# Score bursts of three slots over six PSUM banks, tied into the second MLP layer of two batches ahead, and all eight banks for the first layer

**Chip, cores, metric.** One core of a Trainium2 chip. The metric is device time in microseconds (us), median of several runs of the whole kernel; lower is better.

## The reference

```python
# 8 batches, 12 heads, 448 tokens, 64 per head; model width 768, rank 32
q_n, k_n = q / |q|, k / |k|                     # per token and head
attn = softmax(q_n @ k_n.T / tau)
x = (attn @ v) with the heads side by side      # 8 x 448 x 768
u = x + (x.T @ U @ V).T                         # low-rank mixing of tokens
out = u + relu(u @ w_ch1) @ w_ch2               # MLP, 768 -> 3072 -> 768
```

## The kernel before

The kernel is written as a list of operations for a small planner. The planner places them in time, engine by engine, with its own estimates of durations, and the instructions are then emitted in that order. So each engine's order is fixed when the kernel is built. TensorE has several streams with priorities; the MLP is the last and fills what the others leave. Tokens of the 8 batches are cut into tiles of 128 that are shared between two batches, so even batches have three tiles in the MLP (384 columns in the first layer) and odd ones four (512).

PSUM has eight banks, handed out by rings. A ring is a list of bank groups in order of preference and the number of groups it may hold at a time:

```python
r_mm = bank_ring([(7,), (6,), (5,), (4,)], 3)        # MLP, transposes, U^T x, V^T products
r_av = bank_ring([(5,), (6,), (7,), (4,)], 2, (4, D + 8))   # attention times values
r_sc = bank_ring([(0, 1), (2, 3)], 2)                # scores: a slot of two heads takes two banks
```

A pair of heads has four slots (112 keys each). Scores go in bursts of two slots, that is, four matmuls: the two heads lie in the upper and the lower 64 rows and run side by side.

```python
BURST = 2
for c0 in range(0, SC, g):                           # SC = 4; g = 1 in batch 0, else BURST
    scs = [Slot(r_sc, ...) for _ in range(g)]
    def score():
        for n, sc in enumerate(scs):
            for hh in range(2):
                r = slice(D * hh, D * hh + D)        # 64 rows
                nc.tensor.matmul(out=sc.tile[:, hh, 0:S], lhsT=flat[r, ...], rhs=qkT.tile[r, ...])
    # ... then one exponential on ScalarE per slot, then attention times values per head
```

U^T x comes in two halves of the columns, four matmuls of 32 output columns each, side by side in the array; V^T products and the addition of x follow on VectorE. The MLP:

```python
for f in range(24):                                  # first layer: 6 matmuls into one bank
    mm = Slot(r_mm, 1)
    # ... relu on ScalarE or VectorE empties the bank
for group in groups:                                 # second layer: 24 matmuls into one bank
    mms = [Slot(r_mm, 1) for _ in group]             # batch 0: first three outputs at once
    # ... VectorE adds u and empties the bank
```

## Time and profile before

| | before |
|---|---|
| median time | 598.7 us |
| span of the profiled run | 597.0 us |
| TensorE busy | 586.4 us (98%) |
| score matmuls (L620), all batches | 384 |
| ScalarE, VectorE busy | 46%, 52% |

TensorE is the bound.

### The profile page before, as it was taken

Reading aid. Unit: us, or ns where it says so; the run is one execution under the profiler, and the core shown is the slowest. Engines: PE = TensorE matmul, PEld = TensorE weight load, DVE = VectorE, ACT = ScalarE, POOL = GpSimd, SP = SyncE. Lnnn points to the kernel's source line nnn. Section 1 sums busy time; section 2 is a strip of 40 time slices with the busy share of each in tenths; the row PEclk is TensorE's granted clock in tenths of the full one; section 3 lists DMA queues with packets and bytes.
Section 4 is the critical chain, followed back from the end, with each engine's and each line's share of the span. In section 5 each row is a group of like instructions: output and inputs, shape, how many; then the busy total and the mean of one; then the engine's idle time right before and its main releaser. Section 6 shows DMA issues by size and latency. Waiting matters only on the chain.

```text
span 597.0 us, 11650 instructions
## 1 busy us (share of the span) xinstructions
PE 586.4 (98%) x4878; PEld 329.4 (55%) x4878; DVE 308.8 (52%) x730; ACT 272.0 (46%) x441; POOL 73.7 (12%) x98
## 2 busy tenths in 40 slices
PE   7999999999999999999999999999999999999997
PEld 5555555544555555554445665556445666654565
DVE  6969849999988678658773354124401210110011
ACT  7977653566644566556563046704541025014300
POOL 7234220041300110030020000000000000000000
PEclk9999999999999999999999999999999999999999
DMA  9999995897895695795394121041003110310021
GB/s 154 200 206 192 209 134 112 97 137 110 77 159 101 92 105 72 133 129 94 50 78 97 53 56 22 14 80 33 10 0 63 45 40 1 94 40 1 1 53 54
DMA packets 132852, 50.68 MB, mean 85 GB/s; under 512 B 97728, under 2 KB 132800, under 8 KB 132800
## 3 DMA queue, kind: packets, MB, share of 16 engines
q0 software_dynamic: 71680, 25.73, 38.9%
q1 hardware_dynamic: 61056, 24.19, 21.1%
q8 instruction: 38, 0.62, 0.5%
q14 instruction: 14, 0.11, 0.1%
q10 hardware_dynamic: 64, 0.02, 0.0%
HBM read 52.25 MB, written 11.01 MB: 106 GB/s over the span
## 4 chain that ended last, share of the span: by engine, by line
PE 92%; DVE 3%; ACT 3%; DMA 1%; issue 0%; POOL 0%; ACTq 0%; POOLq 0%
PE bank L850 37%; PE bank L816 36%; PE bank L647 8%; PE bank L620 7%; ACT attn L628 2%; PE bank L740 1%; DMA qk_nat<-in_k_dram 1%; PE bank L448 1%; PE bank L704 1%; DVE xn L573 1%; DVE u_nat L754 1%; DVE O_sb L859 0%; DVE relu L841 0%; ACT sq L499 0%; DVE u_nat L751 0%
## 5 line engine op out<-in xcount | busy, mean ns | idle before, releaser
L816 PE MATMUL bank<-uT,w_sb 128*128 128x512 bf16 (+1 forms) x1152 | 233.2, 353 | 1.9 <-ACT uT L880 0.6
L850 PE MATMUL bank<-w_sb,relu 128*128 128x384 bf16 (+1 forms) x1368 | 231.0, 323 | 0.4 <-DVE O_sb L859 0.3
L633 ACT ACTIVATE attn<-bank 112x896 bf16<-112x896 f32 x176 | 152.6, 920 | 123.8 <-PE bank L620 84.1
L850 PEld LDWEIGHTS <-relu 128*128 128x128 bf16 x1368 | 129.3, 98 | 92.5 <-issue 12.8
L816 PEld LDWEIGHTS <-w_sb 128*128 128x128 bf16 x1152 | 108.4, 98 | 113.5 <-issue 20.4
L839 ACT ACTIVATE relu<-bank 128x512 bf16<-128x512 f32 (+1 forms) x139 | 75.6, 545 | 130.7 <-PE bank L816 128.8
L859 DVE TENSOR_TENSOR O_sb<-bank,u_nat 128x384 f32<-128x384 f32 (+1 forms) x57 | 31.1, 548 | 186.3 <-PE bank L850 161.9
L505 DVE TENSOR_REDUCE ss<-sq 112x8 f32<-112x512 bf16 x96 | 62.6, 672 | 2.4 <-ACT sq L499 2.2
L647 PEld LDWEIGHTS <-attn 112*128 112x128 bf16 x1536 | 55.7, 97 | 10.3 <-issue 3.3
L573 DVE TENSOR_TENSOR xn<-qk_nat,inv 112x512 bf16<-112x512 bf16 x91 | 59.1, 677 | 0.1
L620 PE MATMUL bank<-qkT 64*128 64x448 bf16 x384 | 58.1, 354 | 1.0 <-ACT qkT L880 0.5
L647 PE MATMUL bank<-v_nat,attn 112*128 112x65 bf16 x1536 | 58.6, 193 | 0.1
L841 DVE TENSOR_SCALAR relu<-bank 128x384 bf16<-128x384 f32 (+1 forms) x53 | 32.8, 619 | 35.9 <-PE bank L816 33.8
L656 DVE TENSOR_TENSOR X_sb<-bank,rd 128x256 bf16<-128x256 f32 x96 | 39.0, 416 | 1.5
L479 POOL DMA_DIRECT2D v_nat<-in_v_dram x32 | 29.8, 937 | 61.7 <-PE bank L647 49.2
L470 POOL DMA_DIRECT2D qk_nat<-in_q_dram x24 | 17.2, 718 | 156.1 <-DVE xn L573 132.9
L501 DVE TENSOR_TENSOR sq<-qk_nat 112x512 bf16<-112x512 bf16 x89 | 34.0, 412 | 0.0
L654 DVE RECIPROCAL rd<-bank 128x4 f32<-128x4 f32 x96 | 16.7, 176 | 29.2 <-PE bank L647 28.3
L754 DVE TENSOR_TENSOR u_nat<-bank,X_sb 128x384 bf16<-128x384 f32 (+2 forms) x45 | 22.5, 525 | 15.3 <-PE bank L740 14.9
L620 PEld LDWEIGHTS <-qkT 64*128 64x128 bf16 x384 | 12.0, 94 | 21.9 <-issue 18.5
L628 ACT ACTIVATE attn<-bank,inv 112x448 bf16<-112x448 f32 x32 | 17.4, 656 | 0.7 <-DVE inv L527 0.7
L470 POOL DMA_DIRECT2D qk_nat<-in_k_dram x24 | 16.8, 700 | 4.8 <-DMA w_sb<-in_moe_w_ch_dram 3.6
(52 smaller groups left out, 159.7 us busy)
## 6 DMA issues: line engine op xcount, KB each, us to landing
v_nat<-in_v_dram POOLq DMA_DIRECT2D x32, 168.0 KB, 6.2
qk_nat<-in_q_dram POOLq DMA_DIRECT2D x23, 224.0 KB, 6.5
qk_nat<-in_k_dram POOLq DMA_DIRECT2D x23, 224.0 KB, 7.5
w_sb<-in_moe_w_ch_dram POOLq DMA_DIRECT2D x4, 1152.0 KB, 21.0
w_sb<-in_moe_w_ch_dram POOLq DMA_DIRECT2D x8, 576.0 KB, 15.9
out_dram<-O_sb SPq DMA_DIRECT2D x15, 168.0 KB, 2.3
out_dram<-O_sb SPq DMA_DIRECT2D x16, 144.0 KB, 2.1
out_dram<-O_sb SPq DMA_DIRECT2D x16, 120.0 KB, 2.0
```

Of the source, the lines that this page charges most:

```text
L470: ops = [load(lambda i=i, src=src: nc.gpsimd.dma_start(out=ld.tile[:, i, lo:lo + h1 - h0, :], in_=src[b, h0:h1].rearrange("h (s c) d -> s ...
L501: nc.vector.tensor_mul(y, x, x)
L505: lambda i=i, a0=a0, a1=a1, sq=sq: nc.vector.reduce_sum(ss.tile[:, i, a0:a1, :].rearrange("p h c -> p (h c)"), sq.tile[:, 0:a1 - a0, :].re ...
L573: nc.vector.tensor_mul(dst, src, sc)
L620: nc.tensor.matmul(out=sc.tile[:, hh, 0:S], lhsT=flat[r, SCH * (c0 + n):SCH * (c0 + n) + 128], rhs=qkT.tile[r, SC:2 * SC, :].rearrange("p ...
L633: exps.append(plan.add(Op("ACT", act_t(2 * S, 0.08), lambda sc=sc, c=c0 + n: nc.scalar.activation(out=attn.tile[:, c, :, off:off + S], in_ ...
L647: nc.tensor.matmul(out=av.tile[:, t, 0:D + 1], lhsT=attn.tile[:, j, hh, 128 * t:128 * (t + 1)], rhs=v_t[b % 2][:, h, j, 0:D + 1], start=(j ...
L656: muls.append(plan.add(Op("DVE", dve_t(256), lambda av=av, rd=rd, h=h: nc.vector.tensor_mul(X.tile[:, :, h * D:(h + 1) * D], av.tile[:, :, ...
L816: o = plan.add(Op("PE", pe_t(n), lambda cc=cc: nc.tensor.matmul(out=mm.tile[:, 0:n], lhsT=w1_sb[:, cc, f * 128:(f + 1) * 128], rhs=uT.tile ...
L839: nc.scalar.activation(out=relu.tile[:, f, 0:n], in_=mm.tile[:, 0:n], func=AF.Relu)
L841: nc.vector.tensor_relu(out=relu.tile[:, f, 0:n], in_=mm.tile[:, 0:n])
L850: nc.tensor.matmul(out=mm.tile[:, 0:c1 - c0], lhsT=relu.tile[:, f, i * 128:(i + 1) * 128], rhs=w2_t[:, f, c0:c1], start=(f == 0), stop=(f ...
```

## The change

The intent is to enter the narrow modes of TensorE less often and to give the first MLP layer all banks. (Narrow are scores, on 64 of the 128 rows of the array, and U^T x, on 32 of its 128 columns; going in or out is called a mode change below, and the time that it loses a drain.)

```diff
-    BURST = 2
+    BURST = [1] + [2] * 2 + [3] * 5
+    SPOTS = {8: [(6,)] * 8, 6: [(5, 17), (10,), (5, 17), (10,), (6,), (6,)]}
-    r_sc = bank_ring([(0, 1), (2, 3)], 2)
+    r_sc = bank_ring([(0, 1), (2, 3), (4, 5)], 3)
+    r_low = bank_ring([(5,), (4,), (3,), (2,), (1,), (0,)], 2)
+    r_av2 = bank_ring([(5,), (4,), (3,), (2,), (1,), (0,)], 2, (4, D + 8))
+    r_up = bank_ring([(7,), (6,), (5,), (4,), (3,), (2,), (1,), (0,)], 4)
+    plan.keep = pe_sc, r_sc, (0, 1, 2, 3, 4, 5)      # a ready burst of three reserves these banks
 ... first layer
-                    early[g] = Slot(r_sc1 if b == 0 and f == 0 else r_mm, 1)
+                    early[g] = Slot(r_sc1 if b == 0 and f == 0 else r_up if b >= 0 else r_mm, 1)
 ... second layer
-            mms = [Slot(r_mm, 1) for _ in group]
+            mms = [Slot(r_up if b == 0 else r_mm, 1) for _ in group]
+        todo = bursts.get(b + 2, ())                  # a burst of batch b+2 not before this matmul
+        spots = [(g, f) for g in range(len(downs)) for f in SPOTS[len(downs)][g]] if todo else ()
+        for o, (g, f) in zip(todo, spots):
+            o.deps.append(downs[g][f])
 ... U^T x, batches 2 to 7: both halves in one operation
+        if not by_pe:
+            o = plan.add(Op("PE", 0.2 + 2 * pe_t(CH), project_all, deps=muls + consts[:2 + par], acq=mms + [A]), pe_a)
```

Batches 3 to 7 thus have 8 bursts of six matmuls in place of 12 of four; their V^T products and U^T x use `r_low`, their values `r_av2`. (Cut: the splitting of `attention` into `scores` and `values`, which lets a burst span two pairs.)

More of the change, by code (lines that the diff above doesn't have):

```diff
@@ L40, in __init__ @@
     def __init__(self, n):
-        self.at, self.held = [0.0] * n, {}
+        self.at, self.kept, self.by = [0.0] * n, (), None
 class BankRing(Ring):
@@ L51, in when @@
     def when(self, group):
+        if self.banks.by is not self and any(x in self.banks.kept for x in group):
+            return None
         at = [self.banks.at[x] for x in group]
@@ L91 @@
 class Op:
-    __slots__ = ("eng", "dur", "fn", "deps", "acq", "rel", "prio", "lat", "start", "end", "by", "seq", "fast", "safe")
+    __slots__ = ("eng", "dur", "fn", "deps", "acq", "rel", "prio", "lat", "big", "start", "end", "by", "seq", "fast", "safe")
     def __init__(self, eng, dur, fn, deps=(), acq=(), rel=(), prio=0, lat=0.0, fast=False):
@@ L96, in __init__ @@
         self.deps, self.acq, self.rel = [d for d in deps if d is not None], acq, rel
-        self.start = self.end = self.by = None
+        self.big, self.start, self.end, self.by = False, None, None, None
 class Plan:
@@ L109 @@
     safe = 0.25
+    keep = None
     LAG = {"PE": 0.16, "ACT": 0.10, "DVE": 0.07, "POOL": 0.0, "SP": 0.0}
@@ L188, in run @@
                     pick = None
+                    if e == "PE" and self.keep is not None:
+                        s, ring, kept = self.keep
+                        i = heads[e][self.streams[e].index(s)]
+                        ring.banks.kept, ring.banks.by = (), ring
+                        if i < len(s) and s[i].acq:
+                            new = [x for x in s[i].acq if x.i is None and not isinstance(x.ring, BankRing)]
+                            room = [x.ring.free_at(new[:n].count(x.ring)) for n, x in enumerate(new)]
+                            if all(d.end is not None and d.end <= t for d in s[i].deps) and all(
+                                    x is not None and x <= t for x in room):
+                                ring.banks.kept = kept if s[i].big else ()
                     if e in heads:
@@ L565, in norm @@
         first = b == 0 and p == 0
-        xn, qkT = Slot(r_xn, 2 if by_pe and (first or (b, p) not in RAW_KEYS) else 1), Slot(r_qkT, SC // (1 if b == 0 else BURST))
+        xn, qkT = Slot(r_xn, 2 if by_pe and (first or (b, p) not in RAW_KEYS) else 1), Slot(r_qkT, SC if b == 0 else len({(SC * p + c) // BURST[b] for c in range(SC)}))
         def part(i):
@@ L603, in norm, with scores @@
         return list(ops.values())
-    def attention(b, p, X):
+    attns, bursts = {}, {}
+    def scores(b, slots):
         off = PAD * (b % 2)
-        qkT, qdeps, (inv, a, scaled) = got.pop((b, p, "qkT"))
-        attn = Slot(r_attn, 2)
-        exps = []
-        g = 1 if b == 0 else BURST
-        for c0 in range(0, SC, g):
-            scs = [Slot(r_sc, 2 if (b, p) in RAW_KEYS else 1) for _ in range(g)]
-            def score(scs=scs, c0=c0):
-                flat = qkT.tile.rearrange("p b s -> p (b s)")
-                for n, sc in enumerate(scs):
-                    for hh in range(2):
-                        r = slice(D * hh, D * hh + D)
-                        nc.tensor.matmul(out=sc.tile[:, hh, 0:S], lhsT=flat[r, SCH * (c0 + n):SCH * (c0 + n) + 128],
-                                         rhs=qkT.tile[r, SC:2 * SC, :].rearrange("p c s -> p (c s)"),
-                                         start=True, stop=True)
-            o = plan.add(Op("PE", (0.2 + pe_t(S) * g), score,
-                            deps=qdeps, acq=scs, rel=[qkT]), pe_first if b == 0 else pe_sc)
-            for n, sc in enumerate(scs):
-                if (b, p) in RAW_KEYS:
-                    for hh in range(2):
-                        exps.append(plan.add(Op("ACT", act_t(S, 0.08), lambda sc=sc, c=c0 + n, hh=hh: nc.scalar.activation(
-                            out=attn.tile[:, c, hh, off:off + S], in_=sc.tile[0:SCH, hh, 0:S], func=AF.Exp,
-                            scale=inv.tile[:, 1, a + hh, c:c + 1]), deps=[o, scaled], acq=[attn],
-                            rel=[sc, inv], prio=0.1)))
-                    continue
-                exps.append(plan.add(Op("ACT", act_t(2 * S, 0.08), lambda sc=sc, c=c0 + n: nc.scalar.activation(
-                    out=attn.tile[:, c, :, off:off + S], in_=sc.tile[0:SCH, :, 0:S], func=AF.Exp),
-                    deps=[o], acq=[attn], rel=[sc], prio=0.1 if b == 0 else 1)))
@@ new lines, in scores @@
+        scs = [Slot(r_sc, 2 if (b, p) in RAW_KEYS else 1) for p, _ in slots]
+        sets = {p: got[b, p, "qkT"] for p, _ in slots}
+        ready = []
+        for x in sets.values():
+            ready += x[1]
+        for p in sets:
+            attns.setdefault((b, p), (Slot(r_attn, 2), []))
+        def score():
+            for (p, c), sc in zip(slots, scs):
+                qkT = sets[p][0]
+                flat = qkT.tile.rearrange("p b s -> p (b s)")
+                for hh in range(2):
+                    r = slice(D * hh, D * hh + D)
+                    nc.tensor.matmul(out=sc.tile[:, hh, 0:S], lhsT=flat[r, SCH * c:SCH * c + 128],
+                                     rhs=qkT.tile[r, SC:2 * SC, :].rearrange("p c s -> p (c s)"),
+                                     start=True, stop=True)
@@ new lines, in scores @@
+        o = plan.add(Op("PE", 0.2 + pe_t(S) * len(slots), score, deps=ready, acq=scs + [attns[b, p][0] for p in sets],
+                        rel=[x[0] for x in sets.values()]), pe_first if b == 0 else pe_sc)
+        o.big = len(slots) > 2
+        if o.big:
+            bursts.setdefault(b, []).append(o)
+        for (p, c), sc in zip(slots, scs):
+            _, _, (inv, a, scaled) = sets[p]
+            attn, exps = attns[b, p]
+            if (b, p) in RAW_KEYS:
+                for hh in range(2):
+                    exps.append(plan.add(Op("ACT", act_t(S, 0.08), lambda sc=sc, c=c, hh=hh, attn=attn, inv=inv, a=a: nc.scalar.activation(
+                        out=attn.tile[:, c, hh, off:off + S], in_=sc.tile[0:SCH, hh, 0:S], func=AF.Exp,
+                        scale=inv.tile[:, 1, a + hh, c:c + 1]), deps=[o, scaled], acq=[attn],
+                        rel=[sc, inv], prio=0.1)))
+                continue
+            exps.append(plan.add(Op("ACT", act_t(2 * S, 0.08), lambda sc=sc, c=c, attn=attn: nc.scalar.activation(
+                out=attn.tile[:, c, :, off:off + S], in_=sc.tile[0:SCH, :, 0:S], func=AF.Exp),
+                deps=[o], acq=[attn], rel=[sc], prio=0.1 if b == 0 else 1)))
@@ L636, in attention, with values @@
+    def values(b, p, X):
+        off = PAD * (b % 2)
+        attn, exps = attns.pop((b, p))
         last_exp[b] = exps[-1]
@@ L641, in attention @@
             h = 2 * p + hh
-            av, rd = Slot(r_av, 1), Slot(r_rd, 1)
+            av, rd = Slot(r_av2 if BURST[b] > 2 else r_av, 1), Slot(r_rd, 1)
             for t in range(4):
@@ L691, in stage0 @@
         par = b % 2
-        bank = r_sc1 if b == 1 else r_mm
+        bank = r_sc1 if b == 1 else r_low if BURST[b] > 2 else r_mm
         by_pe = b < PE_BATCHES
@@ L698, in stage0, with project, project_all @@
         ut = []
-        for c0, c1 in cols:
-            mm = Slot(bank, 1)
+        mms = [Slot(bank, 1) for _ in cols]
+        def project(t, c0, c1, mm):
+            nc.tensor.matmul(out=mm.tile[R * t:R * (t + 1), 0:c1 - c0], lhsT=U_sb[:, par, t, :],
+                             rhs=X.tile[:, t, c0:c1], start=True, stop=True)
+        def project_all():
+            for (c0, c1), mm in zip(cols, mms):
+                for t in range(4):
+                    project(t, c0, c1, mm)
+        if not by_pe:
+            o = plan.add(Op("PE", 0.2 + 2 * pe_t(CH), project_all, deps=muls + consts[:2 + par], acq=mms + [A]), pe_a)
+        for (c0, c1), mm in zip(cols, mms):
             need = [m for i, m in enumerate(muls) if i * D < c1]
-            for t in range(4):
+            for t in range(4) if by_pe else ():
                 o = plan.add(Op("PE", pe_t(c1 - c0) + 0.2 if t == 0 else 0.01,
-                                lambda t=t, c0=c0, c1=c1, mm=mm: nc.tensor.matmul(
-                    out=mm.tile[R * t:R * (t + 1), 0:c1 - c0], lhsT=U_sb[:, par, t, :],
-                    rhs=X.tile[:, t, c0:c1], start=True, stop=True),
+                                lambda t=t, c0=c0, c1=c1, mm=mm: project(t, c0, c1, mm),
                     deps=need + consts[:2 + par] if t == 0 else (), acq=[mm, A] if t == 0 else [],
@@ L843, in mlp @@
             done.append(plan.add(r))
+        downs = []
         for group in groups:
-            mms = [Slot(r_mm, 1) for _ in group]
-            last = {}
+            mms = [Slot(r_up if b == 0 else r_mm, 1) for _ in group]
+            last, line = {}, []
             for f in range(NC):
@@ L854, in mlp @@
                         acq=mms if f == 0 else [], rel=[relu] if f == NC - 1 else []), pe_mlp)
+                    line.append(last[mm])
+            downs.append(line)
             for (i, t, c0, c1), mm in zip(group, mms):
@@ L928, in att @@
         muls = [] if b else list(muls0)
+        slots = [(p, c) for p in range(0 if b else 1, NPAIR) for c in range(SC)]
+        step = BURST[b]
+        if b:
+            for n in range(0, len(slots), step):
+                scores(b, slots[n:n + step])
         for p in range(0 if b else 1, NPAIR):
-            muls += attention(b, p, X)
+            if b == 0:
+                for c in range(SC):
+                    scores(b, [(p, c)])
+            muls += values(b, p, X)
         last_mul.extend(muls)
@@ L944 @@
     X0 = Slot(r_X, 0)
-    muls0 = attention(0, 0, X0)
+    for c in range(SC):
+        scores(0, [(0, c)])
+    muls0 = values(0, 0, X0)
     begun_2 = stats(0, 2, 4, *second, hold=begun[:2], then=begun)
```

## The prediction

> **What bounds the kernel now.** I read the page first, then the chain of work in order of time, then the timeline of TensorE, then stretches of time. The page, parts 1, 2 and 4:
>
> ```profile
> PE 586.4 (98%) x4878; PEld 329.4 (55%) x4878; DVE 308.8 (52%) x730; ACT 272.0 (46%) x441; POOL 73.7 (12%) x98
> ...
> DVE  6969849999988678658773354124401210110011
> ...
> PEclk9999999999999999999999999999999999999999
> ...
> PE 92%; DVE 3%; ACT 3%; DMA 1%; issue 0%; POOL 0%; ACTq 0%; POOLq 0%
> ```
>
> TensorE is busy 98% of the span, at full clock, and is 92% of the chain that ends last. So no transfer and no other engine can give much back; only work or lost time on TensorE itself counts. Whether it loses time inside its "busy" is seen where nothing disturbs it, in the last pieces of the chain (start, length, what):
>
> ```profile
> 484.48 23.40 PE bank L816 x144
> 507.88 23.40 PE bank L850 x144
> 531.28 31.08 PE bank L816 x144
> ```
>
> A 384-column matmul costs 23.40/144 = 162.5 ns there, a 512-column one 31.08/144 = 215.8 ns. Two points give 0.4167 ns a column plus 2.5 ns, so 448 columns (one head's scores of one slot) should cost 189.2 ns. Now the same layer with attention in it, from the timeline of TensorE (start, length of the merged piece, which overlaps its neighbour because ends are modelled; so I take start to start):
>
> ```profile
> 316.63 0.55 PE L620 MATMUL bank<-qkT 64*128 64x448 bf16 x4
> 317.11 3.10 PE L850 MATMUL bank<-w_sb,relu 128*128 128x384 bf16 x18
> 320.14 0.55 PE L620 MATMUL bank<-qkT 64*128 64x448 bf16 x4
> 320.63 3.10 PE L850 MATMUL bank<-w_sb,relu 128*128 128x384 bf16 x18
> 323.66 0.55 PE L620 MATMUL bank<-qkT 64*128 64x448 bf16 x4
> ```
>
> One burst of scores to the next takes 3.51 us. The 18 second-layer matmuls between are 18 x 0.1625 = 2.925, so a burst costs 0.59. It holds two slots of two heads; the two heads lie in different halves of the rows and run side by side, so its streaming is 2 x 0.189 = 0.378. The other **0.21 us is lost per burst**, at its entry and exit, whatever its length. The same for U^T x:
>
> ```profile
> 181.99 0.55 PE L620 MATMUL bank<-qkT 64*128 64x448 bf16 x4
> 182.47 1.64 PE L850 MATMUL bank<-w_sb,relu 128*128 128x384 bf16 x9
> 184.04 0.35 PE L704 MATMUL bank<-X_sb,U_sb 128*32 128x384 bf16 x4
> 184.32 1.31 PE L850 MATMUL bank<-w_sb,relu 128*128 128x384 bf16 x7
> 185.56 0.55 PE L620 MATMUL bank<-qkT 64*128 64x448 bf16 x4
> ```
>
> Burst to burst 3.57, less 0.59 for the first burst, less 16 x 0.1625 = 2.60, leaves 0.38 for one half of U^T x. Its four matmuls lie side by side in four column strips and stream in 0.1625, so about 0.21 is lost here too.
>
> **What the Trainium skill says.** (1) "TensorEngine Tiling (Array Packing)", section Tiling Modes, Key Properties: changing the tiling mode drains TensorE, changing the tile within a mode does not. The trace agrees: 64x128 (scores) and 128x32 (U^T x) amid 128x128 lose 0.21 us each, while the attention-by-values runs (L647, 128 columns) lose nothing comparable at entry. (2) "TensorE: Matmul & The Clock Gate", section Back-to-back issue gap: N/2.4 + 2.5 ns in a warm stream; 162.5 and 215.8 ns agree to 0.1 ns. (3) "PSUM — Partial Sum Buffer", Specifications: 8 banks of 512 fp32. So a slot of two heads at 448 columns takes two banks, and three slots take six, leaving two for the MLP; the trace does not show bank numbers. (4) "Perfetto Trace Analysis", section Identifying the Most-Contended Engine: matmul busy share is a poor measure of nearness to the limit. The 98% agrees: it includes the drains.
>
> **The change part by part.**
>
> *Scores in threes.* Batches 3 to 7 have 24 slots each: 12 bursts before, 8 after. Matmuls, exponentials and columns are the same. The burst becomes 0.21 + 3 x 0.189 = 0.78 us; 8 x 0.78 = 6.2 a batch against 12 x 0.59 = 7.1. Over five batches 20 drains of 0.21: **-4.2 us**, all on TensorE, which sets the end.
>
> *One U^T x burst.* Batches 2 to 7: 12 half bursts become 6, six drains less, 1.3 us. But in the timeline some 5 of the 12 halves stand directly beside a score burst and so share a drain (305.07 U^T x, then 305.35 scores). A shared one costs about 0.1 less, and I do not expect the new bursts at the end of a batch to find such neighbours: -1.3 + 5 x 0.1 = **-0.8 us**.
>
> *Tied to the second layer of two batches ahead.* This only moves work. The exponentials set the pace of the bursts:
>
> ```profile
> L633 ACT ACTIVATE attn<-bank 112x896 bf16<-112x896 f32 x176 | 152.6, 920 | 123.8 <-PE bank L620 84.1
> ```
>
> Three take 3 x 0.92 = 2.76 us. A second layer with a batch of attention in it lasts: 144 x 0.1625 = 23.4 (three token tiles) or 31.2 (four), plus 6.2 for scores, plus about 6 x 1.1 = 6.6 for values (228.93 to 230.05 for one pair), so 36 or 44 us. That is a burst each 4.5 or 5.5 us. ACT carries 22 us in it, 50 to 60%. It fits and costs nothing. Batch 7's attention moves from about 416-431 to about 452-484 us; its result is needed at 531 us. No end wait.
>
> *All eight banks for the first layer.* Score banks no longer stand in the first layer's way once batch 3 has begun. After 100 us TensorE waits for something only in one place; stretches (length, then busy of each engine):
>
> ```profile
> 112.30:154.70 42.40, 42.40 (x350) 20.23 (x349) 40.34 (x94) 28.09 (x48) 9.31 (x12) 1.00 1.08 118
> 154.70:200.80 46.10, 46.10 (x447) 26.80 (x446) 37.44 (x91) 22.60 (x34) 7.91 (x10) 1.00 0.91 119
> 200.80:237.20 36.40, 35.64 (x328) 20.07 (x327) 28.05 (x67) 23.67 (x39) 6.52 (x8) 1.00 0.90 82
> ```
>
> The 0.76 us in the third stretch ends with releases by VectorE (u_nat L751 and L754, near 212 and 215 us): V^T products and first-layer results fill four banks while a late VectorE empties them. I give this **-0.5 us**. Against it, new waits of a denser second layer: **+0.5 us**.
>
> *The start.* Until 38 us ScalarE's exponentials of batch 0 and the loads set the pace. A third score slot there would need bank 4, which the warm-up tile holds until batch 0's U^T x. Scores now also wait for their attention buffer; three buffers are there and values of earlier pairs are done by then. I take **0**, with perhaps 0.5 either way.
>
> Sum: -4.2 - 0.8 - 0.5 + 0.5 = -5.0 us; 598.7 - 5.0 = **593.7 us**, 0.8% faster.
>
> **The rivals.**
>
> *(A) The wait moves to PSUM.* A burst of three needs six empty banks at once, so the last exponential of the previous burst must be done. TensorE's order is fixed when the kernel is built, from durations in the planner: 0.08 + 896 x 0.00083 = 0.82 us for an exponential that measures 0.92. A burst may thus come 0.3 us early, against a margin of 0.8 us in the plan. For it: no second chance, since TensorE works in order. Against it: ACT is only half loaded there, and before the change not one score burst after 100 us waited. If a quarter of the 40 bursts waited 0.3 us: +3 us, 596.7.
>
> *(B) VectorE becomes the bound of a stretch.* It is busy 40.3 of 42.4 us at 112-155 and 37.4 of 46.1 at 155-201. Batch 3's attention now starts no sooner than 155, so normalising later batches, paced by the six transposed-key buffers, is put off too. For good: the packed stretch thins out and the waits of 94-101 and 212-215 us go; 592. For bad: values, normalising and the layer's results meet on VectorE in second layers; +2 us, 595.7.
>
> *(C) The drains are hidden anyway.* If TensorE waited for something else behind them, taking 20 away would give little: about 597.5. Against it: the chain is TensorE itself and idle before its matmuls sums to about 1 us after 100 us.
>
> *(D) The drain grows with the burst* (six weight loads in the narrow mode instead of four). Were half a drain added per burst, 40 x 0.1 = 4 us would eat the gain. Against it: within a burst the second slot starts 0.2 us after the first, near its streaming time of 0.189.
>
> **Range and chances.** (A) and the bad half of (B) set the upper edge, the good half of (B) with a full 1.3 us for U^T x and a better start the lower: 590.5 to 597.0. Over 2% would need 586.7 or less, 12 us: the drains of all 60 bursts of these batches together are 12.6, and two thirds of them stay. So faster by over 2% has 0.03, slower by over 2% (12 us of new waits) 0.02, within 2% 0.95.
>
> **What would show each step right or wrong.** Right: score matmuls of batches 3 to 7 in pieces of x6, about 0.68 us start to start with the following layer, 40 of them; 0.78 us lost to the 162.5 ns stream; none between first-layer matmuls after 201 us; U^T x in pieces of x8, about 0.55 us; exponentials between 452 and 484 us, where there are none now; TensorE idle after 100 us still about 1 us. Wrong: idle before score matmuls released by ACT attn (A); TensorE idle in second layers released by VectorE (B); pieces of x6 lasting over 0.8 us (D); a start that ends later than the first full first-layer run at 42.45 us. The prediction fails if the start shifts by more than 1 us or if waits of over 3 us appear.

## The result, and the profile after

589.87 us median (589.62 to 590.12, 4 runs) against 598.75 before (598.34 to 598.92, 4 runs); ratio 0.9853, 95% interval 0.9836 to 0.9870. A ratio is the mean time of one kernel's fast runs over that of the other's of the same rounds, so not quite the ratio of the medians. The kernel is 8.9 us faster, not 5.0, and below the predicted range.

The page of the kernel after, parts 1 and 4, in the same order as before:

```profile
PE 580.2 (99%) x4878; PEld 329.1 (56%) x4878; DVE 298.1 (51%) x711; ACT 281.8 (48%) x460; POOL 73.6 (13%) x98
...
PE 95%; ACT 3%; DVE 1%; DMA 1%; issue 0%
```

VectorE's part of the chain fell from 3% to 1%. One per cent of the span is 6 us, so waits for VectorE may have gone as well as drains; how much, these rounded shares do not say.

The timeline of TensorE in a second layer of the kernel after (scores are L643, second layer L892, values L679):

```profile
298.28 0.74 PE L643 MATMUL bank<-qkT 64*128 64x448 bf16 x6
298.96 2.29 PE L892 MATMUL bank<-w_sb,relu 128*128 128x384 bf16 x13
301.08 1.19 PE L679 MATMUL bank<-v_nat,attn 112*128 112x65 bf16 x32
302.11 2.11 PE L892 MATMUL bank<-w_sb,relu 128*128 128x384 bf16 x12
304.15 0.74 PE L643 MATMUL bank<-qkT 64*128 64x448 bf16 x6
```

Burst to burst 5.87 us, less 25 x 0.1625 = 4.06 for the second layer and 302.11 - 301.08 = 1.03 for the values, leaves 0.78 for a burst of three, as predicted. U^T x, the same kernel:

```profile
150.95 2.32 PE L857 MATMUL bank<-uT,w_sb 128*128 128x512 bf16 x10
153.20 0.51 PE L734 MATMUL bank<-X_sb,U_sb 128*32 128x384 bf16 x8
153.65 0.39 PE L857 MATMUL bank<-uT,w_sb 128*128 128x512 bf16 x1
```

From 150.95 to 153.65 are 2.70 us; ten 512-column matmuls stream in 2.16; the eight of U^T x cost 0.54, as expected.

What TensorE waited for, from the view of waits of the kernel before (line that waited, releaser: total us, times, longest); the lines of the MLP and of V^T products:

```profile
PE bank L816 <- ACT uT L880: 0.6, 1, 0.6
PE bank L816 <- DVE qkT L882: 0.5, 1, 0.5
PE bank L816 <- DVE u_nat L751: 0.5, 1, 0.5
...
PE bank L850 <- DVE O_sb L859: 0.3, 1, 0.3
...
PE bank L816 <- DVE u_nat L754: 0.3, 1, 0.3
...
PE bank L740 <- DVE u_nat L754: 0.2, 1, 0.2
```

and after, where of the same lines one is left (near 42 us, at the first layer's beginning):

```profile
PE bank L857 <- ACT uT L929: 0.6, 1, 0.6
```

**A count over the whole trace.** To see what is behind the modelled ends, I took the start of every matmul to the start of the next and subtracted its stream cost of N/2.4 + 2.5 ns (a pair or a strip group counted once). After 39.5 us, when the first full first layer begins, what is left falls into three parts. Changes of mode: between two matmuls of which one is a score or a U^T x and the other is not, about 0.1 us each (the entry 0.096, the exit 0.092; into and out of U^T x 0.094 and 0.106). Waits: over 0.05 us elsewhere. And the rest, which is small and nearly the same in all.

| trace | mode changes | their sum | waits | start to 39.5 us, lost | end |
|---|---|---|---|---|---|
| before | 197 | 18.8 us | 4.6 us | 13.6 us | 593.6 us |
| after | 151 | 14.3 us | 0.9 us | 13.5 us | 584.9 us |

So of 8.7 us, 4.9 are the 46 mode changes (4.5 plus 0.4 of the slightly slow first matmuls behind them, together **0.107 us a change**), 3.7 are waits that are gone, 0.1 is the start. The waits of before stood in many places: 56, 66, 71, 78, 95 and 100 us (2.0 us together) and 125, 142, 212, 215, 260 and 435 us (1.7). After, only those at 41 and 42 us are left, which both kernels have.

### The profile page after: what moved, and what is told of

The parts are those of the page before. It is cut to its first block, busy times and chain, and to the rows that moved or that the text cites.

```text
span 588.3 us, 11676 instructions
## 1 busy us (share of the span) xinstructions
PE 580.2 (99%) x4878; PEld 329.1 (56%) x4878; DVE 298.1 (51%) x711; ACT 281.8 (48%) x460; POOL 73.6 (13%) x98
## 4 chain that ended last, share of the span: by engine, by line
PE 95%; ACT 3%; DVE 1%; DMA 1%; issue 0%
PE bank L892 38%; PE bank L857 38%; PE bank L679 8%; PE bank L643 8%; ACT attn L656 2%; PE bank L781 2%; PE bank L466 1%; PE bank L734 1%; ACT sq L517 1%; DMA raw_uv<-in_q_dram 1%; ACT qkT L929 0%; DVE ss L523 0%; PE bank L715 0%; PE bank L827 0%; PE bank L710 0%
## 5 line engine op out<-in xcount | busy, mean ns | idle before, releaser
L892 PE MATMUL bank<-w_sb,relu 128*128 128x384 bf16 (+1 forms) x1368 | 232.1, 323 | 0.0
L661 ACT ACTIVATE attn<-bank 112x896 bf16<-112x896 f32 x176 | 149.9, 920 | 98.9 <-PE bank L643 98.5
L892 PEld LDWEIGHTS <-relu 128*128 128x128 bf16 x1368 | 128.3, 98 | 92.6 <-issue 15.1
L880 ACT ACTIVATE relu<-bank 128x384 bf16<-128x384 f32 (+1 forms) x164 | 88.6, 541 | 138.5 <-PE bank L857 138.0
L679 PEld LDWEIGHTS <-attn 112*128 112x128 bf16 x1536 | 55.9, 97 | 11.3 <-issue 3.6
L679 PE MATMUL bank<-v_nat,attn 112*128 112x65 bf16 x1536 | 59.1, 193 | 0.1
L643 PE MATMUL bank<-qkT 64*128 64x448 bf16 x384 | 54.6, 353 | 1.5 <-ACT qkT L929 0.6
L643 PEld LDWEIGHTS <-qkT 64*128 64x128 bf16 x384 | 13.6, 94 | 26.7 <-issue 21.0
L882 DVE TENSOR_SCALAR relu<-bank 128x512 bf16<-128x512 f32 (+1 forms) x28 | 18.0, 641 | 9.5 <-PE bank L857 9.1
```

What stands on the lines that cost most here:

```text
L643: nc.tensor.matmul(out=sc.tile[:, hh, 0:S], lhsT=flat[r, SCH * c:SCH * c + 128], rhs=qkT.tile[r, SC:2 * SC, :].rearrange("p c s -> p (c s) ...
L661: exps.append(plan.add(Op("ACT", act_t(2 * S, 0.08), lambda sc=sc, c=c, attn=attn: nc.scalar.activation(out=attn.tile[:, c, :, off:off + S ...
L679: nc.tensor.matmul(out=av.tile[:, t, 0:D + 1], lhsT=attn.tile[:, j, hh, 128 * t:128 * (t + 1)], rhs=v_t[b % 2][:, h, j, 0:D + 1], start=(j ...
L880: nc.scalar.activation(out=relu.tile[:, f, 0:n], in_=mm.tile[:, 0:n], func=AF.Relu)
L892: nc.tensor.matmul(out=mm.tile[:, 0:c1 - c0], lhsT=relu.tile[:, f, i * 128:(i + 1) * 128], rhs=w2_t[:, f, c0:c1], start=(f == 0), stop=(f ...
```

## Experiments

My theory now: the drains paid what the prediction said; the other 3.7 us came from the eight banks for the first layer. Rivals: the waits went because attention left the first layers (the tie), or because of the third pair of score banks. In the table, waits of the runs marked * are what is left of the end time after the start, the mode changes at 0.1065 us and a constant (554.46 us, from the kernel before); their traces lack some 20 matmul records, which a direct sum would take for waits. Where no record is missing the two ways agree to 0.1 us.

| run | median us | ratio to before (95%) | mode changes | waits us |
|---|---|---|---|---|
| before | 598.3 to 598.8 | 1 | 197 | 4.6 |
| after | 589.9 | 0.985 (0.984 to 0.987) | 151 | 0.9 |
| a_u_halves | 591.4 | 0.988 (0.986 to 0.990) | 162 | 0.9 |
| a_four_banks | 592.5 | 0.990 (0.988 to 0.991) | 151 | 3.0 |
| a_twos_tied | 595.8 | 0.996 (0.994 to 0.997) | 191 | 1.9 |
| a_untied | 591.5 | 0.989 (0.987 to 0.990) | 151 | 2.4 |
| b_eight_banks* | 595.4 | 0.995 (0.993 to 0.996) | 200 | 1.2 |
| b_six_score_banks* | 597.7 | 0.998 (0.997 to 1.000) | 198 | 3.5 |
| b_both* | 595.8 | 0.996 (0.994 to 0.997) | 199 | 1.8 |
| b_ones* | 606.2 | 1.013 (1.011 to 1.014) | 275 | 3.6 |
| b_four_open* | 598.0 | 0.999 (0.997 to 1.000) | 202 | 3.5 |
| b_eight_three* | 596.7 | 0.997 (0.995 to 0.998) | 200 | 2.4 |

### a_u_halves: U^T x in two halves again

```diff
-        if not by_pe:
-            o = plan.add(Op("PE", ..., project_all, ...), pe_a)
-            for t in range(4) if by_pe else ():
+            for t in range(4):
```

> The changed kernel with U^T x of batches 2 to 7 in two half bursts again. Theory 'drains' (each entry and exit of a narrow-mode burst loses 0.2 us on TensorE, nothing hides it): 12 pieces of x4 in place of 6 of x8, six drains more where none stands beside a score burst, 0.6 to 1.3 us, so 590.5 to 591.2 us. Rival 'hidden' (drains lie behind other waits): 589.9. No new TensorE idle.

591.4 us, 1.5 more than the changed kernel. 11 mode changes more and not a tenth of a microsecond of new waits; the end in the trace is 1.23 us later. The theory of drains holds, just above its range (591.2): hardly any of the new halves shared a drain.

### a_four_banks: the first layer on four banks again

```diff
-    Slot(r_sc1 if b == 0 and f == 0 else r_up if b >= 0 else r_mm, 1)
+    Slot(r_sc1 if b == 0 and f == 0 else r_mm, 1)
-            mms = [Slot(r_up if b == 0 else r_mm, 1) for _ in group]
+            mms = [Slot(r_mm, 1) for _ in group]
```

> The changed kernel with the first layer, and batch 0's group of three, back on four banks with three open. What the prediction missed is 3.7 us of waits before matmuls that are gone (2.0 before 112 us, 1.7 after). Theory 'eight banks' (first-layer results waited for banks that late VectorE had not emptied): the waits before 112 us come back, 591.5 to 593 us, TensorE loses 1.5 us or more in first-layer waits. Rival 'attention moved' (waits went because scores and values are out of first layers, or because batch 1 has three score slots): stays at 589.9 with no waits.

592.5 us, within the range of 'eight banks': the number of mode changes is the same 151, and 2.1 us of waits are back, all but 0.3 before 101 us. The largest, 0.8 us at 78 us, stands before batch 0's group of three in the second layer; before first-layer matmuls it is 0.6 us, less than the 1.5 expected. The view of waits of this run has lines of MLP matmuls that wait for VectorE, which the changed kernel lacks:

```profile
PE bank L892 <- DVE relu L882: 0.6, 1, 0.6
...
PE bank L857 <- DVE relu L882: 0.2, 1, 0.2
```

But only 0.3 of the 1.7 us after 112 us came back. There four banks suffice, either because attention is out of the first layers or because values, U^T x and V^T products of batches 3 to 7 stay on the low banks (`r_av2`, `r_low`), which this run keeps too; no run separates the two.

### a_twos_tied: bursts of two in the same places

```diff
-    BURST = [1] + [2] * 2 + [3] * 5
+    BURST = [1] + [2] * 7
+    SPOTS = 12 places in place of 8
-        o.big = len(slots) > 2
+        o.big = b > 2            # still tied, still reserving six banks; r_low and r_av2 kept
```

> The changed kernel with bursts of two in batches 3 to 7, still tied to the second layer of two batches ahead (12 places in place of 8) and still reserving the six banks. Theory 'drains': 20 score bursts more, 20 x 0.21 = +4.2 us, 594.1 us, waits as in the changed kernel (about 1 us after 39 us). Rival 'placing is what pays' (the gain comes from attention out of first layers): about 590.5. If waits come back too: 596 or more.

595.8 us. The 40 mode changes more (20 bursts) are there, and 40 x 0.107 = 4.3 us. Another 0.9 us of waits came (0.6 at 161 us). The profiled span is 5.3 us longer than the changed kernel's (593.6 against 588.3), which these two account for; the other 0.7 us lies outside the trace (time of a run less its span is 2.2 us here and 1.8 there, and the medians stand differently to the profiled runs). So of the gain of the changed kernel the longer bursts are the largest single part. Placing bursts of two is worth little: with the eight banks and the whole U^T x this run is 2.9 us faster than before, and eight banks alone bring that (below).

### a_untied: bursts of three anywhere

```diff
-        todo = bursts.get(b + 2, ())
+        todo = ()
```

> The changed kernel with bursts of three not tied to any place: they go where exponentials and buffers let them, in first layers too. Theory 'drains and eight banks': the number of bursts is the same (64 after 39 us), so 589.9 to 590.4. Rival 'the tie removes waits': 0.5 to 2 us of waits near 200 to 220 us come back, 590.5 to 592.

591.5 us: 151 mode changes as in the changed kernel, 1.5 us of waits more, at 153 (0.85 us), 170 and 226 us. The rival holds in size, though not in place. The first wait ends with a relu on ScalarE. From the timeline of this run:

```profile
150.56 1.72 ACT L661 ACTIVATE attn<-bank 112x896 bf16<-112x896 f32 x2
...
152.21 0.38 PE L857 MATMUL bank<-uT,w_sb 128*128 128x512 bf16 x1
152.63 0.60 ACT L880 ACTIVATE relu<-bank 128x512 bf16<-128x512 f32 x1 [0.35 <-PE bank L857]
...
153.28 1.46 PE L857 MATMUL bank<-uT,w_sb 128*128 128x512 bf16 x6 [0.68 <-ACT relu L880]
```

The bracket is the idle time before the piece and its releaser. The relu did not stand behind exponentials: the two before it ended at 152.28, and ScalarE sat idle for 0.35 us until TensorE had finished the result. The next matmul of the first layer had no bank until that relu had emptied this one. Why is in the kernel's planner, which can be run without the chip and whose order of all 4737 matmuls (the warm-up's left out) is the trace's: the burst of three before took banks 0 to 5, and as its exponentials free them they stay reserved for the next burst, which is ready; values of batch 2 took bank 6, and the first layer is left with bank 7. So the tie does not only move work: keeping bursts of three and their reserved banks out of the first layers is worth about 1.6 us.

### b_eight_banks, b_six_score_banks, b_both: parts of the change alone, on the kernel before

```diff
+    r_up = bank_ring([(7,), (6,), (5,), (4,), (3,), (2,), (1,), (0,)], 4)   # b_eight_banks, b_both
+    first layer and batch 0's group of three take r_up in place of r_mm
-    r_sc = bank_ring([(0, 1), (2, 3)], 2)                                   # b_six_score_banks, b_both
+    r_sc = bank_ring([(0, 1), (2, 3), (4, 5)], 3)
```

> The kernel before with one part of the change: first layers (and batch 0's group of three) may use all eight banks, four open. Undoing this in the changed kernel brought 2.1 us of waits back, all but 0.3 of it before 112 us. Theory 'eight banks': the 2.0 us of waits before 112 us go, those at 212 and 215 us (1.1 us) perhaps too; drains as before (197 mode changes after 39 us): 595.7 to 597 us. Rival 'only together with the rest' (the banks are taken by scores as long as attention runs in first layers): 598.2 or more.

> The kernel before with a third pair of score banks for every batch, bursts of two as they were. Theory 'eight banks': scores take banks from the first layer and remove no wait and no drain: 598 to 600 us. Rival 'score slots' (first batches' scores waited for slots): waits before 112 us shrink, 597 us.

> Both parts, nothing tied, bursts of two, two half bursts of U^T x. If banks alone remove the waits: 595.5 to 597 us, the same as eight banks alone. If it needs both: clearly below it.

Eight banks alone: 595.4 us, 2.9 less than before and 0.3 below the expected range, with no mode change fewer: waits fall from 4.6 to 1.2 us, in both halves of the kernel. Of the first layer (L817 in this run) the view of waits has two lines left, and of the second layer none:

```profile
PE bank L817 <- issue: 1.6, 10, 0.2
...
PE bank L817 <- ACT uT L881: 0.6, 1, 0.6
```

"issue" stands where one 512-column matmul is missing from the trace (gaps of 0.22 us). Apart from such gaps, start to start leaves 0.9 us at 41 and 42 us and 0.2 us each at 58 and 432 us. Nothing else of the change is in this run, so this is shown: **the first layer's banks alone remove nearly all of the waits that the prediction missed.** The third pair of score banks alone brought 0.6 us, between its two expectations, with waits down by 1.1; the interval reaches to 0.9999, so a small gain. Both together (595.8) are no better than eight banks alone. Each of the two, eight banks (here) and what a_four_banks keeps (the tie and the low banks), is enough for the waits after 112 us; for those before 101 us it needs the banks.

### b_four_open, b_eight_three: number of banks, or number open?

```diff
+    r_up = bank_ring([(7,), (6,), (5,), (4,)], 4)                           # b_four_open
+    r_up = bank_ring([(7,), (6,), (5,), (4,), (3,), (2,), (1,), (0,)], 3)   # b_eight_three
```

> The kernel before with first layers on their old four banks but four of them open in place of three. Eight banks with four open took 2.9 us off. Theory 'number open' (TensorE only needed one more result in flight): about 595.5 us, waits of 1 us. Theory 'other banks' (results and V^T products held the four banks, and a fifth to eighth was needed): little, 597.5 to 598.5 us, waits over 2.5 us.

> The counterpart: eight banks, three open as before. Theory 'other banks': about 595.5 us with waits of 1 us. Theory 'number open': 597.5 to 598.5 us.

Neither theory alone. Four open on four banks saved 0.8 us, with an interval that just includes no change (1.0001); 0.5 of its waits' gain went into five more mode changes. Eight banks with three open saved 2.1, both 2.9. The place matters more than the number; by the rings of the code, results, transposes and V^T products no longer compete for the same four.

### b_ones: single slots in batches 3 to 7

```diff
-        g = 1 if b == 0 else BURST
+        g = 1 if b == 0 or b > 2 else BURST
```

> The kernel before with bursts of one slot in batches 3 to 7: 60 score bursts more. Theory 'drains', the same per burst whatever its length: 60 x 0.2 = +12 to 12.6 us, 610.7 to 611.3 us, less about 0.1 us for each burst that comes to stand beside another narrow piece. If the loss grew with the length (rival D of the prediction: half per slot), single slots would lose less each and the sum would be about +6, 605 us.

606.2 us, 7.9 more. This is near the number of the rival, but not for its reason. Singles often came to stand side by side, so only 41 score pieces and 78 mode changes more appeared in the trace, not 60 and 120. 78 x 0.107 = 8.3. That sum cannot test the price, since the waits of this run are what it leaves over. Start to start can: from the matmul before a piece of scores to the one after it, less the streaming, the median loss is 0.202 us with one slot (74 pieces of this run), with two (78 of the kernel before) and with three (40 of the changed kernel). So a drain that grows with the burst is excluded.

### c_b2, c_b1b2, c_b2_up: can more bursts go in threes?

```diff
-    BURST = [1] + [2] * 2 + [3] * 5
+    BURST = [1, 2] + [3] * 6       # c_b2 (c_b1b2: [1] + [3] * 7); batch 2 is not tied
```

> The changed kernel with batch 2 in bursts of three as well (not tied to a place). 8 mode changes fewer in TensorE's order at 0.107 us each: -0.85 us, 589.0 us, if no wait is added. Rival: batch 2 runs while VectorE is over 90% busy and inside a first layer, so emptying six banks at once brings waits of 0.5 to 2 us, 589.5 to 591 us.

> The changed kernel with batches 1 and 2 in bursts of three. 21 mode changes fewer: -2.2 us, 587.7 us, if no wait is added. Rival as for batch 2 alone, more so, since batch 1 also shares banks with batch 0's first layer and transposes: waits of 1 to 3 us take it back, 589 to 591 us.

599.5 us (ratio 1.002, 1.001 to 1.003) and 613.2 us (1.025, 1.023 to 1.026): both expectations missed by far. The drains fell as counted, but TensorE ran out of work. (A batch in threes also reserves the six banks and moves to the low rings, so these runs change three things at once.) Timeline of TensorE in c_b2:

```profile
191.82 0.81 PE L643 MATMUL bank<-qkT 64*128 64x448 bf16 x4 [0.82 <-DVE X_sb L688]
195.68 1.61 PE L679 MATMUL bank<-v_nat,attn 112*128 112x65 bf16 x32 [3.05 <-ACT attn L661]
...
201.17 1.14 PE L857 MATMUL bank<-uT,w_sb 128*128 128x384 bf16 x3 [1.97 <-DMA uT<-u_nat]
```

and stretches of it (length; busy of PE, PEld, DVE, ACT, POOL; granted clock; transfers):

```profile
190.00:206.00 16.00, 10.05 (x72) 4.07 (x69) 14.41 (x37) 8.35 (x16) 0.00 (x0) 0.69 0.62 107
206.00:220.00 14.00, 14.00 (x168) 9.34 (x167) 8.41 (x21) 5.56 (x11) 5.13 (x6) 0.99 0.60 39
```

Batch 2's U^T x comes at 178.0 us here, at 153.2 in the changed kernel. Its u is transposed too late for the first layer at 201 us; with the MLP, TensorE's filler is gone, and every wait is exposed. The granted clock, a mean of 0.69 over these 16 us, is 0.50 from 196.1 to 206.4 us and 1.00 before and after: 384-column matmuls start 0.32 us apart from 201 to 206 us, twice 0.1625. It fell just after the idle 3.05 us, before the 1.97. The Trainium skill, "TensorE: Matmul & The Clock Gate", section HAM oscillation, warns of idle gaps of over about 3.4 us; the trace agrees in kind, though the gaps before the fall are shorter: 0.82 and 3.05 us.

To see whether the reserved low banks kept batch 2's U^T x out, I gave it any of the eight:

```diff
-        bank = r_sc1 if b == 1 else r_low if BURST[b] > 2 else r_mm
+        bank = r_sc1 if b == 1 else r_low if b > 2 else r_up
```

> Batch 2 in threes as in the run before, but its U^T x may take any of the eight banks in place of the six low ones that the score bursts reserve. Theory 'reserve starves U^T x' (batch 2's projection waits for banks that batch 3's bursts hold or reserve, so the first layer of mlp 2 starts late): most of the 10 us comes back, 590.5 to 593.5 us, and TensorE's waits between 190 and 205 us fall from over 8 us to 1 to 4 us, without a fall of the granted clock. Rival 'batch 2 is late in itself' (VectorE and exponentials): stays at 597 us or more.

594.8 us: neither range. U^T x still comes at 178.8 us, so the banks did not hold it up and my theory falls; yet the waits shrank (2.3 us at 194 and 0.9 at 196 us are the largest) and the clock fell less, to a mean of 0.83 over 186 to 206 us (0.50 from 193.4 to 200.2, so it fell inside the gap of 2.3 us). What makes batch 2 late when its bursts span two pairs, and why its later steps went faster here, stays open. No version beat the changed kernel.

## Why the prediction was wrong

- **What bounds the kernel, the price of a drain, the 0.78 us of a burst of three, the 0.54 of a whole U^T x: right.** Score bursts after 39.5 us fell from 84 to 64 and pieces of U^T x from 18 to 12. Predicted for both together -5.0 us, measured -4.9 (40 changes of scores 4.3, six of U^T x 0.6).
- **The start: right** (0 predicted, -0.1).
- **The step that failed is "All eight banks for the first layer", with its -0.5 us and the +0.5 us set against it.** They measured -3.7 us and nothing, and eight banks alone take 3.4 of it (waits of 4.6 and 1.2 us). The mechanism that it named, few banks that a late VectorE empties, was right; the size was not. Two faults made it small. First, I looked after 100 us only, "TensorE waits for something only in one place"; 2.0 us of waits stood between 56 and 101 us, in the first layer and the group of three of batch 0, which the change also gives all banks (the diff says `b == 0` for the group), and 0.3 of it before a V^T product of batch 1. Second, I took the idle time that the profile shows. It counts from modelled ends and is shorter than what is lost: at 212 us the profile shows 0.49 us idle where start to start loses 0.65, and waits of under 0.2 us do not show at all. Part 4 of the page had the warning: VectorE had 3% of the chain, and the prediction priced 0.5 us of it.
- **"This only moves work" and costs nothing: half right.** It costs nothing, but without it 1.5 us of waits come back (a_untied). The tie keeps bursts of three, which hold or reserve six banks, out of the first layers.
- **Rival (A)** did not happen in the changed kernel: no score matmul waited after 42 us. (Untied, a wait for PSUM did come, on the side of the first layer.) Its figure was wrong too: the 0.92 us of an exponential is its latency. Eight in a row took 6.67 us in the kernel before, 0.83 each, which is what the planner assumes:

```profile
30.48 6.67 ACT L633 ACTIVATE attn<-bank 112x896 bf16<-112x896 f32 x8
```

- **Rival (B)**, its good half, is what happened in effect: the waits named there went, and 592 was named for it. I weighed it as an edge, and gave VectorE's packed stretch as the cause; eight banks alone do it with VectorE's work unchanged. **(C)** and **(D)** fell, (D) by the same 0.202 us for one, two and three slots.
- Of the signs, 40 pieces of six matmuls came. "TensorE idle after 100 us still about 1 us" failed: the profile shows none. Batch 7's exponentials ran from 431.6 to 472.1 us, earlier than the 452 to 484 named, without effect.
- The chances were right in that the gain stays under 2%.

## What to carry to other kernels

On a saturated TensorE, add up start-to-start times less the stream cost over the whole trace, early part included, before pricing a change; the busy share and the shown idle time hide both drains and short waits. Price a burst in another tiling mode by its entry and exit, not its length. Make bursts longer only where banks and the supply of other work allow it: batch 2 in threes cost 9.6 us, batches 1 and 2 together 23.3. When a change frees buffers, list every wait that ends with the release of such a buffer: here that was worth three quarters as much as the saving that the change was built for.

## What the Trainium skill lacked or had wrong

- "TensorEngine Tiling (Array Packing)", Tiling Modes, Key Properties, says that a change of mode drains TensorE but gives no figure: 0.107 us a change here, 0.21 us for in and out, the same for bursts of one, two and three slots (151 to 275 changes).
- "TensorE: Matmul & The Clock Gate", section Back-to-back issue gap, gives about 131 ns per 512-column matmul for a sustained stream of weight load and matmul. Here each of 144 such matmuls with its own weight load took 215.8 ns, which is its formula for a single gap.
- "Perfetto Trace Analysis", Per-instruction lifecycle, says that TensorE's ends are estimated; it does not say that shown idle time is therefore too short: 0.49 us shown where 0.65 us was lost.
- "TensorE: Matmul & The Clock Gate", section HAM oscillation, puts the danger at idle gaps of over about 3.4 us; the next section, "A second HAM failure mode: psum-queue depth-cycling", lets frequent short idling do it too, but gives no length. Here the granted clock fell to 0.50 for 10.2 us after gaps of 0.82 and 3.05 us (c_b2), and for 6.8 us inside a gap of 2.29 us (c_b2_up).
